# A new engine order for attention with beacon keys and a two-layer MLP, from a planner with longer delays for the beacon keys

## The chip, the cores and the metric

The kernel runs on one core of a Trainium2 chip. What counts is the device time of one execution in microseconds; of several executions of one kernel the median is taken. A profile is one further execution, recorded by the hardware profiler.

## The reference, cut to what matters

Eight batches of eight heads attend over 576 tokens of width 64. In front of the keys and values stand 16 beacon keys and values that every query sees; the rest is causal. The attention's output, 4608 tokens of width 512, goes through two dense layers with a sigmoid-gated unit between them.

```python
k_all = np.concatenate([beacon_k, k], axis=2)
v_all = np.concatenate([beacon_v, v], axis=2)
scores = scale * np.matmul(q, k_all.transpose(0, 1, 3, 2))
causal[:, Nb:] = np.triu(np.ones((S, S), dtype=bool), k=1)
scores = np.where(causal, -1000000000.0, scores)
scores = scores - scores.max(-1, keepdims=True)
a = np.exp(scores)
a /= a.sum(-1, keepdims=True) + 1e-09
x = np.matmul(a, v_all)              # then (tokens, 512)
h = x @ w_in                         # (4608, 512) @ (512, 2048)
g = h * (1.0 / (1.0 + np.exp(-1.702 * h)))
out = g @ w_out                      # (4608, 2048) @ (2048, 512)
```

All inputs are float32 and are turned to float16 as they are loaded; the output is float32.

## The kernel before, in words

**Steps.** Four heads of one batch make a step `s`; there are 16 steps, two for each batch. A step loads its q and k (GpSimd DMA, L349), turns both on VectorE so that the head's width lies on partitions (`e_turn`: L398 for the beacon keys, L405 for k and q), multiplies them in chunks on TensorE (`qk`, L434), takes exps on ScalarE (L445), sets what causality hides to zero on GpSimd or VectorE (L466, L459), multiplies with a matrix of ones and with the values (`av`, L521), and divides by the sums on VectorE (z1 L533, z2 L540 and L544, norm L556). Steps 0 and 1 are early steps: their chunks are cut so that a first half of the tokens is done before the second. There is one score tile, so a chunk's matmuls wait for the exps of the chunk before. All other PSUM results share a ring of four banks.

**Beacon keys.** They are float32 in `bkf`, which is set to zero first, then filled by DMAs of SyncE (a few of ScalarE for step 0), and cast for each step into `bkn` by VectorE (`e_bk`, L390). The loads for step 0 and step 1 are issued at once. Those for steps 2 and 3, 4 to 7 and 8 to 15 each follow a memset (L1072, operations 82, 87 and 92 of the plan), and are four DMAs each. SyncE also issues the output's stores, all in one order.

**Dense layers.** Tokens go in groups of 256 or 512. The first layer (`m1`, L580) is followed by tanh and a gate (L594, L613) in groups 0 and 1, by one activation (L601) later. The second layer is plain in groups 0 and 1 (`m2`, L625). Groups 2 to 9 form seven products of quarter matrices (L694) from sums of quarters made on VectorE (`s`, L645) and join them (L705, L710). The weights are loaded in pieces by GpSimd, at most eight of its loads in flight at a time.

**The order.** Nothing is scheduled at run time. The kernel makes a list of operations, each with an engine, a planned duration and dependencies. `ORDER`, a table of numbers, gives for each engine the order in which its operations stand. `Plan.run` walks through the table with planned durations and delays (`Plan.lat`) and so decides which ring bank each result gets and in which order the code is emitted. The table comes from a search made beforehand with the same durations and delays. Each engine works through its list in order and waits where a dependency isn't met.

The numbers that matter here. TensorE: 76, 100, 106, 108, 111, 129, 131, 134 are `qk0` to `qk7` (steps 0 and 1), 227 is `qk8`, the first of step 2; 115, 118, 120 are the values of step 0, first half, and 138, 141, 143 those of step 1; 122, 125, 127 and 145, 148, 150 are the second halves; 152, 155, 158 and so on are first-layer blocks of group 0; 176 and 177 the first second-layer blocks. VectorE: 73, 97, 224, 255, 398, 411 cast the beacon keys of steps 0 to 5; 74 and 75 turn k and q of step 0, 98 and 99 those of step 1, 225 and 226 those of step 2; 82, 87, 92 are the memsets; 126 and 128 are norms of step 0's second half, 149 and 151 of step 1's; 347 is the first join of group 2.

Of the kernel before, what the change touches and what calls it, by code (L numbers as in the profile page):

```python
# [17 lines left out]
        76, 100, 115, 118, 120, 106, 138, 143, 141, 108, 152, 111, 155, 158, 129, 161, 122, 164, 131, 167, 170, 134,  # L18
        127, 125, 173, 176, 145, 148, 150, 177, 182, 188, 191, 227, 194, 197, 183, 232, 203, 200, 234, 178, 179,
        237, 184, 206, 258, 241, 209, 185, 263, 212, 213, 265, 248, 253, 251, 246, 268, 214, 215, 401, 218, 272,  # L20
        279, 244, 404, 277, 219, 220, 407, 282, 284, 275, 221, 414, 312, 292, 306, 435, 308, 316, 302, 310, 320,
        304, 300, 290, 296, 294, 298, 318, 314, 423, 426, 343, 338, 339, 349, 344, 340, 341, 345, 438, 346, 431,
        429, 433, 464, 350, 365, 351, 359, 360, 574, 354, 355, 356, 352, 361, 577, 366, 357, 477, 362, 367, 583,
        474, 368, 372, 373, 374, 605, 480, 482, 484, 375, 607, 488, 504, 498, 610, 494, 516, 486, 490, 496, 500,
        492, 510, 508, 506, 512, 502, 514, 593, 596, 534, 535, 539, 536, 545, 540, 537, 546, 550, 742, 551, 552,
        541, 542, 547, 745, 599, 548, 603, 601, 619, 622, 748, 553, 555, 561, 556, 557, 755, 558, 562, 625, 627,
        629, 776, 563, 564, 568, 569, 570, 764, 767, 779, 571, 657, 649, 661, 651, 653, 635, 659, 647, 641, 631,
        637, 805, 770, 772, 774, 633, 643, 645, 639, 655, 684, 690, 679, 685, 680, 686, 681, 682, 915, 815, 818,
        691, 692, 687, 695, 700, 918, 693, 696, 701, 702, 697, 924, 698, 703, 821, 823, 825, 946, 706, 707, 708,
        709, 713, 948, 934, 937, 714, 715, 716, 827, 951, 944, 940, 942, 841, 829, 855, 853, 849, 845, 839, 851,  # L30
        857, 835, 833, 831, 837, 843, 847, 1083, 960, 963, 875, 880, 876, 881, 877, 878, 882, 1086, 970, 966, 968,
        883, 1089, 896, 886, 887, 888, 891, 1096, 892, 893, 902, 894, 889, 1117, 897, 903, 898, 899, 904, 1120, 909,
        910, 905, 911, 1105, 1108, 1146, 912, 986, 992, 994, 990, 976, 982, 974, 988, 1000, 978, 984, 972, 980, 998,
        1002, 996, 1256, 1156, 1115, 1111, 1113, 1159, 1025, 1026, 1020, 1021, 1022, 1023, 1259, 1031, 1027, 1028,
        1166, 1162, 1164, 1265, 1032, 1033, 1041, 1034, 1042, 1043, 1287, 1036, 1037, 1038, 1039, 1044, 1289, 1275,
        1278, 1054, 1055, 1047, 1048, 1049, 1050, 1056, 1292, 1281, 1283, 1285, 1057, 1198, 1196, 1182, 1168, 1184,
        1172, 1170, 1178, 1174, 1176, 1180, 1188, 1190, 1301, 1304, 1194, 1192, 1216, 1186, 1307, 1221, 1222, 1223,
        1339, 1217, 1218, 1227, 1224, 1228, 1229, 1219, 1232, 1230, 1337, 1243, 1233, 1237, 1238, 1234, 1239, 1244,
        1235, 1240, 1245, 1246, 1309, 1311, 1250, 1319, 1251, 1329, 1252, 1325, 1335, 1321, 1315, 1253, 1419, 1323,
        1411, 1423, 1421, 1331, 1343, 1333, 1313, 1415, 1341, 1403, 1429, 1409, 1361, 1362, 1363, 1364, 1413, 1327,  # L40
        1317, 1407, 1417, 1401, 1366, 1367, 1431, 1405, 1388, 1368, 1369, 1427, 1382, 1383, 1425, 1377, 1378, 1389,
        1372, 1373, 1374, 1390, 1391, 1375, 1384, 1385, 1379, 1380, 1395, 1396, 1397, 1454, 1398, 1455, 1470, 1471,
        1456, 1472, 1449, 1473, 1450, 1451, 1452, 1460, 1461, 1462, 1457, 1463, 1465, 1466, 1467, 1468, 1476, 1477,
        1478, 1479, 1483, 1484, 1485, 1486,
    ],
    "ACT": [
        1, 3, 77, 79, 101, 103, 107, 109, 153, 112, 156, 159, 130, 162, 165, 132, 168, 171, 135, 174, 189, 192, 228,
        195, 198, 233, 201, 235, 204, 238, 180, 207, 259, 210, 264, 186, 266, 269, 216, 402, 405, 408, 222, 415,
        417, 293, 309, 313, 303, 311, 307, 305, 317, 291, 321, 297, 301, 295, 299, 319, 315, 436, 342, 439, 465,
        468, 575, 578, 587, 584, 606, 608, 489, 505, 517, 487, 491, 499, 501, 493, 497, 511, 495, 507, 513, 509,  # L50
        503, 515, 611, 538, 743, 746, 749, 756, 758, 777, 780, 658, 650, 654, 662, 636, 660, 652, 632, 642, 638,
        648, 806, 634, 644, 646, 640, 656, 809, 683, 916, 919, 925, 928, 947, 949, 952, 828, 830, 842, 850, 856,
        840, 846, 858, 836, 834, 852, 854, 838, 832, 844, 848, 1084, 879, 1087, 1090, 1099, 1097, 1118, 1121, 1150,
        1147, 987, 991, 993, 995, 983, 975, 1001, 979, 989, 985, 981, 977, 1003, 973, 997, 999, 1257, 1024, 1260,
        1266, 1269, 1288, 1290, 1293, 1199, 1197, 1183, 1169, 1185, 1179, 1171, 1175, 1173, 1177, 1181, 1189, 1191,
        1193, 1195, 1187, 1340, 1220, 1338, 1320, 1326, 1330, 1322, 1336, 1324, 1316, 1412, 1422, 1424, 1332, 1420,
        1344, 1334, 1314, 1404, 1430, 1416, 1342, 1414, 1365, 1318, 1408, 1328, 1418, 1410, 1432, 1402, 1406, 1428,
        1426, 1453,
    ],
    "DVE": [  # L60
        73, 97, 74, 75, 98, 99, 78, 81, 80, 116, 117, 102, 121, 104, 105, 119, 139, 140, 144, 142, 154, 157, 123,
        124, 82, 160, 166, 163, 169, 172, 224, 126, 128, 175, 146, 147, 149, 151, 225, 226, 87, 190, 193, 196, 255,
        199, 256, 257, 205, 202, 411, 286, 398, 208, 287, 242, 211, 243, 399, 249, 400, 250, 252, 254, 247, 92, 412,
        280, 273, 281, 413, 245, 274, 278, 283, 276, 285, 288, 461, 419, 580, 463, 289, 462, 330, 420, 331, 421,
        332, 322, 422, 323, 333, 326, 427, 327, 424, 334, 335, 324, 336, 428, 425, 337, 328, 347, 329, 325, 432,
        430, 470, 434, 582, 471, 472, 473, 353, 581, 358, 478, 363, 475, 476, 479, 369, 370, 481, 483, 485, 589,
        739, 590, 376, 752, 741, 753, 615, 591, 754, 740, 522, 523, 518, 802, 519, 592, 520, 524, 921, 525, 526,
        527, 594, 521, 530, 528, 531, 597, 595, 532, 529, 616, 617, 598, 533, 543, 618, 600, 549, 604, 620, 602,
        623, 554, 621, 624, 760, 559, 761, 628, 762, 630, 763, 626, 565, 768, 566, 765, 572, 769, 811, 812, 803,
        766, 804, 922, 773, 771, 671, 775, 923, 663, 1093, 664, 665, 667, 813, 814, 668, 675, 672, 676, 669, 666,  # L70
        673, 816, 670, 819, 674, 820, 688, 1080, 677, 694, 817, 678, 930, 699, 704, 931, 822, 932, 933, 824, 826,
        710, 935, 938, 939, 936, 711, 717, 945, 943, 941, 956, 957, 958, 1082, 1081, 1094, 959, 1095, 859, 1262,
        863, 871, 860, 864, 865, 961, 867, 964, 965, 962, 872, 861, 868, 873, 869, 971, 866, 884, 1143, 862, 969,
        870, 874, 967, 1101, 1144, 890, 1145, 1102, 1103, 1104, 895, 900, 1109, 1106, 906, 913, 907, 1152, 1153,
        1107, 1263, 1154, 1264, 1012, 1155, 1008, 1110, 1013, 1014, 1009, 1157, 1116, 1016, 1112, 1010, 1004, 1160,
        1114, 1005, 1161, 1006, 1158, 1011, 1017, 1029, 1167, 1018, 1007, 1015, 1019, 1271, 1035, 1272, 1163, 1165,
        1273, 1274, 1040, 1276, 1279, 1045, 1280, 1277, 1051, 1052, 1284, 1286, 1058, 1282, 1297, 1298, 1200, 1299,
        1300, 1204, 1201, 1305, 1205, 1306, 1302, 1303, 1202, 1308, 1206, 1212, 1213, 1208, 1209, 1214, 1203, 1215,
        1225, 1207, 1210, 1211, 1231, 1236, 1241, 1247, 1248, 1310, 1312, 1254, 1357, 1349, 1350, 1345, 1358, 1359,
        1351, 1353, 1360, 1354, 1352, 1355, 1346, 1356, 1347, 1348, 1370, 1376, 1381, 1386, 1392, 1393, 1437, 1441,  # L80
        1433, 1434, 1438, 1399, 1435, 1442, 1445, 1446, 1436, 1443, 1439, 1444, 1440, 1447, 1448, 1458, 1464, 1469,
        1474, 1480, 1481, 1487,
    ],
    "POOL": [
# [32 lines left out]
class Plan:  # L117
# [69 lines left out]
    def lat(self, d, o):  # L187
        if o.eng == "Q":
            return 300 if d.eng == "SP" else 1200
        if d.name == "bk" and d.eng != "DVE":  # L190
            return 2500
# [928 lines left out]
```

## Time and profile before

| | |
|---|---|
| median of three executions | 333.64 us |
| their lowest and highest | 332.74, 335.28 us |
| profiled execution | 336.76 us, of which the span from the first to the last instruction is 335.1 us |
| busy, TensorE matmul | 313.5 us (94%), 4288 instructions |
| busy, VectorE, ScalarE, GpSimd | 234.9 (70%), 201.2 (60%), 112.8 us (34%) |
| DMA | 28.81 MB |

The page names engines PE (TensorE), PEld (its weight loads), DVE (VectorE), ACT (ScalarE), POOL (GpSimd) and SP (SyncE). In its second part the span is cut into 40 slices of 8.4 us; a digit is the busy share in tenths, and the row PEclk is the share of TensorE's clock that was granted. The chain that ended last is followed back from the last instruction. In a timeline, a line gives the start, the length, the engine, the source line and the operation, and in brackets how long the engine had been idle and what ended that. In the list of waits, a line gives who waited for whom, the time in total, how often, and the longest.

The DMA row of the slices is at 9 for most of the first 67 us and seldom later: the inputs of the first steps and all weights are loaded there.

```profile
DMA  7999999939051980199019909810110001000023
```

### The profile page before, as it was taken

What the parts mean: (1) busy time and instruction counts of PE and PEld (TensorE: products, weight loads), DVE (VectorE), ACT (ScalarE), POOL (GpSimd) and SP (SyncE); (2) the same over time, 40 slices, a digit from 0 to 9 for tenths busy, and PEclk for the clock granted to TensorE, in tenths of its full rate; (3) what the DMA queues carried; (4) which work ended last, traced back from release to release, by engine and by line L of the source; (5) the groups of instructions that cost most, each with busy time, mean ns of one, the idle gap of its engine ahead of it and who ended that gap; (6) DMA issues with size and microseconds to landing.
All of it is one profiled execution on the core that took longest, in us unless ns stands there. A gap on an engine that the chain in (4) does not pass through costs nothing. (4 is left out here: it accounts for less than half of the span.)

```text
span 335.1 us, 9823 instructions
## 1 busy us (share of the span) xinstructions
PE 313.5 (94%) x4288; PEld 212.2 (63%) x4288; DVE 234.9 (70%) x478; ACT 201.2 (60%) x236; POOL 112.8 (34%) x178
## 2 busy tenths in 40 slices
PE   0499699999999999999999999999999999999995
PEld 0377376654687457755778877646874586455884
DVE  0755658886999879977897979777983844006294
ACT  1378069876976777577967696767666422645100
POOL 8746537637034803481048108320303000000000
PEclk9999699999999999999999999999999999999999
DMA  7999999939051980199019909810110001000023
GB/s 125 162 205 209 196 98 169 117 85 165 0 106 64 147 101 25 45 138 139 2 67 100 178 3 89 127 59 3 33 65 33 2 31 65 32 0 2 31 97 125
DMA packets 58219, 28.81 MB, mean 86 GB/s; under 512 B 41280, under 2 KB 53568, under 8 KB 58176
## 3 DMA queue, kind: packets, MB, share of 16 engines
q0 software_dynamic: 47552, 18.49, 47.5%
q1 hardware_dynamic: 10560, 9.69, 8.8%
q8 instruction: 33, 0.54, 0.7%
q14 instruction: 10, 0.08, 0.1%
q10 hardware_dynamic: 64, 0.01, 0.0%
HBM read 37.22 MB, written 9.44 MB: 139 GB/s over the span
## 5 line engine op out<-in xcount | busy, mean ns | idle before, releaser
L580 PE MATMUL u<-xT,w 128*128 128x512 f16 (+1 forms) x704 | 131.1, 341 | 0.1
L445 ACT ACTIVATE E<-s 128x2048 f16<-128x2048 f32 (+4 forms) x66 | 98.9, 1514 | 46.5 <-PE s L434 46.3
L580 PEld LDWEIGHTS <-w 128*128 128x128 f16 x704 | 67.8, 98 | 53.6 <-issue 1.0
L601 ACT ACTIVATE g<-u 128x512 f16<-128x512 f32 x128 | 69.8, 599 | 46.1 <-PE u L580 45.9
L466 POOL TENSOR_SCALAR_AFFINE_SELECT E<-E 128x512 f16<-128x512 f16 (+3 forms) x78 | 48.1, 644 | 127.7 <-ACT E L445 118.7
L694 PEld LDWEIGHTS <-g 128*128 128x128 f16 x512 | 48.7, 98 | 7.7
L710 DVE SCALAR_TENSOR_TENSOR osb<-u,osb 128x512 f32<-128x512 f32 x56 | 37.4, 681 | 20.2 <-PE u L694 16.4
L694 PE MATMUL u<-w,g 128*128 128x256 f16 x384 | 49.2, 273 | 0.0
L434 PE MATMUL s<-qT,kT 32*128 32x32 f16 (+20 forms) x1376 | 35.7, 234 | 14.2 <-DVE kT L398 11.2
L434 PEld LDWEIGHTS <-kT 32*128 32x128 f16 x1376 | 26.1, 95 | 30.9 <-issue 13.1
L694 PEld LDWEIGHTS <-sA 128*128 128x128 f16 x384 | 36.1, 98 | 6.1 <-issue 0.2
L694 PE MATMUL u<-tB,sA 128*128 128x256 f16 x256 | 34.3, 273 | 0.0
L645 DVE TENSOR_TENSOR sA<-g 128x512 f16<-128x512 f16 x32 | 13.1, 417 | 28.0 <-ACT g L601 27.9
L521 PE MATMUL u<-E,vb 128*32 128x352 f16 (+8 forms) x928 | 28.9, 273 | 0.0
L556 DVE TENSOR_TENSOR xT<-u,rz 128x352 f16<-128x352 f32 (+2 forms) x52 | 26.0, 518 | 3.1 <-PE u L521 2.5
L365 POOL DMA_DIRECT2D vb<-in_v_dram x32 | 27.4, 875 | 1.6 <-DMA qn<-in_q_dram 0.8
L521 PEld LDWEIGHTS <-vb 128*32 128x32 f16 (+1 forms) x928 | 21.1, 101 | 6.0 <-issue 1.7
L484 DVE TENSOR_TENSOR zs<-zs,E 128x1344 f16<-128x1344 f16 (+2 forms) x36 | 22.5, 626 | 3.0 <-POOL E L466 2.1
L405 DVE STREAM_TRANSPOSE kT<-kn 128x576 f32<-128x576 f32 x16 | 20.1, 1257 | 3.4 <-PE s L434 1.9
L484 DVE TENSOR_TENSOR zs<-E 128x1856 f16<-128x1856 f16 x12 | 15.4, 1282 | 9.4 <-POOL E L466 9.4
L533 DVE STREAM_TRANSPOSE zt<-u 128x224 f32<-128x224 f32 (+2 forms) x32 | 14.8, 473 | 7.6 <-PE u L521 7.4
L405 DVE STREAM_TRANSPOSE qT<-qn 128x576 f32<-128x576 f32 x16 | 19.7, 1234 | 0.0
(44 smaller groups left out, 241.1 us busy)
## 6 DMA issues: line engine op xcount, KB each, us to landing
out_dram<-osb SPq DMA_DIRECT2D x36, 256.0 KB, 2.5
kn<-in_k_dram POOLq DMA_DIRECT2D x16, 288.0 KB, 6.9
qn<-in_q_dram POOLq DMA_DIRECT2D x16, 288.0 KB, 6.8
vb<-in_v_dram POOLq DMA_DIRECT2D x24, 128.0 KB, 5.9
w<-in_moe_w_in_dram POOLq DMA_DIRECT2D x8, 256.0 KB, 8.1
w<-in_moe_w_out_dram POOLq DMA_DIRECT2D x4, 512.0 KB, 13.1
vb<-in_v_dram POOLq DMA_DIRECT2D x8, 112.0 KB, 4.0
vb<-in_v_dram POOLq DMA_DIRECT2D x8, 80.0 KB, 6.9
```

The costliest lines, as they stand in the source:

```text
L365: nc.gpsimd.dma_start(out=t[0 : hi - lo, j, h0:h1, :], in_=v[b, h0:h1, lo:hi, :].rearrange("h n d -> n h d"),)
L405: nc.vector.transpose(out=f32(dst.rearrange("p n e -> p (n e)")).rearrange("p (r t) -> p t r", t=TR), in_=f32(src[:, :]).rearrange("p (t c ...
L434: nc.tensor.matmul(sc[:, h, o : o + w], kT[s % NB2][r : r + 32, j * P : (j + 1) * P, d], qT[s % NB2][r : r + 32, a : a + w, d], start=(d = ...
L445: nc.scalar.activation(out=Es[s][:, :, c0:c1], in_=ss[i][:, :, o : o + c1 - c0], func=AFT.Exp, scale=0.125,)
L466: nc.gpsimd.affine_select(out=blk, in_=blk, compare_op=ALU.is_ge, fill=0.0, base=off + (Nb if j == 0 else 0), pattern=[[0, Q], [1, w]], ch ...
L484: nc.vector.tensor_tensor(out=t, in0=E[:, :, Z0:S] if i == 1 else t, in1=E[:, :, wcol[i] : wcol[i] + S - a], op=ALU.add,)
L521: nc.tensor.matmul(u[32 * h : 32 * h + 32, a:e], lhs, src[0:kw, h, col : col + e - a], start=first, stop=last,)
L556: nc.vector.tensor_tensor(out=xT[:, 2 * hs + x : 2 * hs + x + n, t0 : t0 + w], in0=rings[("av", s, x, half)][:, 0 : n * w].rearrange("p (n ...
L580: nc.tensor.matmul(u[:, o + a - t0 : o + e - t0], w1t[:, kp, nt * P : (nt + 1) * P], xT[:, kp, a % XR : (e - 1) % XR + 1], start=(kp == 0) ...
L601: nc.scalar.activation(out=gts[g][:, n0:n1, 0:w], in_=rings[("m1", g, n0)][:, 0 : n * w].rearrange("p (n w) -> p n w", n=n), func=AFT.Gelu ...
L694: nc.tensor.matmul(u[:, HM * mt : HM * (mt + 1)], lhs[:, n, mt * P : (mt + 1) * P], rhs[:, n, :], start=(n == 0 and mt == 0), stop=(n == H ...
L710: nc.vector.scalar_tensor_tensor(out=osbs[(g, dst)][:, :], in0=rings[("p", g, p)][:, :], scalar=scale_of(g), in1=osbs[(g, src)][:, :], op0 ...
```

## The change

In `Plan.lat`, the planned delay between a load of beacon keys and their cast was 2500 ns for every step. It becomes 2500 for step 0, 5200 for step 1 and 9000 for the later ones. `ORDER` is replaced by a table that the search found with these delays. SyncE's list is the same in both; TensorE's, ScalarE's, VectorE's and GpSimd's differ from the start to the end, with the same operations in each. GpSimd's loads keep their order; its masks swap places with their neighbours. Of the table the first rows of TensorE and VectorE are shown, the rows in which memset 92 stands, and VectorE's last.

```diff
     "PE": [
-        76, 100, 115, 118, 120, 106, 138, 143, 141, 108, 152, 111, 155, 158, 129, 161, 122, 164, 131, 167, 170, 134,
-        127, 125, 173, 176, 145, 148, 150, 177, 182, 188, 191, 227, 194, 197, 183, 232, 203, 200, 234, 178, 179,
+        76, 100, 106, 138, 115, 141, 118, 143, 120, 108, 111, 155, 152, 129, 161, 158, 122, 131, 164, 167, 134, 127,
+        170, 173, 176, 145, 125, 148, 150, 177, 182, 188, 191, 227, 194, 197, 232, 183, 203, 234, 200, 178, 237,
...
     "DVE": [
-        73, 97, 74, 75, 98, 99, 78, 81, 80, 116, 117, 102, 121, 104, 105, 119, 139, 140, 144, 142, 154, 157, 123,
-        124, 82, 160, 166, 163, 169, 172, 224, 126, 128, 175, 146, 147, 149, 151, 225, 226, 87, 190, 193, 196, 255,
-        199, 256, 257, 205, 202, 411, 286, 398, 208, 287, 242, 211, 243, 399, 249, 400, 250, 252, 254, 247, 92, 412,
...
-        1433, 1434, 1438, 1399, 1435, 1442, 1445, 1446, 1436, 1443, 1439, 1444, 1440, 1447, 1448, 1458, 1464, 1469,
-        1474, 1480, 1481, 1487,
+        73, 74, 75, 97, 98, 99, 80, 81, 82, 78, 105, 87, 104, 102, 139, 116, 117, 121, 119, 140, 144, 142, 157, 154,
+        123, 163, 160, 124, 224, 169, 128, 166, 172, 175, 146, 147, 126, 149, 151, 225, 226, 398, 190, 193, 196,
...
+        421, 322, 92, 323, 324, 422, 427, 428, 424, 425, 325, 330, 334, 329, 335, 432, 336, 331, 434, 337, 332, 333,
...
+        1399, 1437, 1434, 1438, 1447, 1435, 1441, 1442, 1436, 1443, 1444, 1439, 1448, 1440, 1458, 1464, 1469, 1480,
+        1474, 1481, 1487,
...
         if d.name == "bk" and d.eng != "DVE":
-            return 2500
+            return {"bk0": 2500, "bk1": 5200}.get(o.name, 9000)
         return self.LAT[d.eng] if o.eng != d.eng or d.eng == "Q" else 0
```

## The prediction

> **What bounds the kernel now.** I began with the page: the busy time of the engines (PE 313.5 of 335.1 us), the slices with the clock row, and the chain that ended last, which is PE alone from 212.75 us on. In the slices the reader is to see that the first two hold idle PE, that the fifth is a 6 in PE's row and in the clock's, and that nothing else is short of 9 before the last slice:
>
> ```profile
> PE   0499699999999999999999999999999999999995
> ...
> PEclk9999699999999999999999999999999999999999
> ```
>
> Sums by stretch say the same: from 42 to 331 us PE is busy 288.39 of 289.00. So time can be won only before 42 us or in the tail of 4 us. Next I asked who PE waited for. Before 40 us there are three entries; after 40 us there is one, of 0.2 us:
>
> ```profile
> PE s L434 <- DVE kT L398: 11.2, 1, 11.2
> PE u L521 <- DVE xT L556: 3.0, 1, 3.0
> PE s L434 <- ACT E L445: 2.8, 3, 2.0
> ```
>
> The releasers of the first two stand in DVE's timeline, and in both places a cast of beacon keys (L390) is the instruction that DVE stood at. The brackets give the idle time before it and what ended it:
>
> ```profile
> 8.51 0.20 DVE L390 CAST bkn<-bkf 128x64 f16<-128x64 f32 x1 [4.68 <-DMA bkf<-in_beacon_k_dram]
> ...
> 9.96 1.23 DVE L405 STREAM_TRANSPOSE qT<-qn 128x576 f32<-128x576 f32 x1
> ...
> 27.92 0.17 DVE L1072 MEMSET bkf<- 128x128 f32 x1
> ...
> 35.78 0.20 DVE L390 CAST bkn<-bkf 128x64 f16<-128x64 f32 x1 [4.36 <-DMA bkf<-in_beacon_k_dram]
> ```
>
> The second place costs more than its wait. PE stands still from 33.3 to 36.4 us and then runs at half clock; the columns after the stretch are its length, PE, PEld, DVE, ACT and POOL busy, granted clock, DMA share and GB/s:
>
> ```profile
> 33.30:35.40 2.10, 0.07 (x1) 0.09 (x1) 0.00 (x0) 0.00 (x0) 2.10 (x3) 1.00 1.14 207
> 35.50:36.40 0.90, 0.01 (x2) 0.01 (x2) 0.62 (x3) 0.00 (x0) 0.46 (x2) 0.50 1.20 204
> 36.40:38.90 2.50, 2.50 (x52) 2.01 (x55) 2.08 (x5) 0.00 (x0) 1.31 (x2) 0.50 1.24 207
> 38.90:42.30 3.40, 3.40 (x23) 1.24 (x15) 3.21 (x5) 0.00 (x0) 0.56 (x1) 0.50 1.89 174
> 42.30:44.40 2.10, 2.10 (x20) 1.58 (x19) 0.55 (x3) 0.60 (x1) 0.00 (x0) 1.00 2.25 173
> ```
>
> PE lost 3.03 us of standstill and half of the 5.9 us from 36.4 to 42.3: 2.95. Together 5.98 us.
>
> **The Trainium skill.** "TensorE: Matmul & The Clock Gate", Part 1: the array's clock is halved by default and after an idle window of about 3.4 us; a busy window of that length restores it; the windows run free of the kernel. The trace agrees: half clock from about 35.4 to 42.3 us is two such windows, and at the start the matmuls are slow (24 of scores 1.04 us at 11.24, 0.54 at 24.51). A stretch from 14.9 to 18.4 us with PE busy 2.86 of 3.50 did not end it, one from 18.4 to 21.8 with 3.24 of 3.40 did. "Perfetto Trace Analysis", Tensor Engine Instruction: VectorE's queue is strictly in order, so what is behind a waiting cast waits too; the norms that release PE at 36.39 do. "DMA: Bandwidth & Descriptors", Issuing engines are not separate DMA queues: SyncE's transfers share 16 engines with GpSimd's. In the trace the first beacon loads land 1.6 to 1.8 us after their issue, the next, behind the loads of q and k, after 3.9 to 5.1, those of 28 us after 4.4 to 6.2.
>
> **The change, part by part.** No instruction is added or removed. The planner's delay between beacon load and cast changes from 2.5 us for all to 2.5, 5.2 and 9 (step 0, step 1, later), and with it the order on PE, ACT, DVE and POOL; SP's order and that of GpSimd's loads among themselves stay.
>
> *Cast of bk1 behind the turns of step 0.* k0 and q0 land at 1.30+4.4=5.7 and 1.96+5.1=7.1 us, so the turn of q0 (1.23 us) ends at about 8.4 instead of 11.2. qk0 starts at 8.5, not 11.24: 2.75 earlier. bk1 (landed 8.39) is then cast with no wait. q1 lands at 2.99+7.6=10.6, its turn ends at 11.9, and qk1 starts at 11.95, not 14.32: 2.37 earlier.
>
> *What PE does with that.* qk2 now comes before the values of half 0, and must wait for the exps of qk1 (1.94 us, one score tile): 11.95+1.04+0.05+1.94 gives 15.0; it ran at 17.40. The six value groups follow; the old ones took 15.29 to 16.76 for three, so 2.85 for six, to 18.9. qk3 runs at 19.05, its exp from 19.9 to 21.4 (1.45). qk4 now stands directly behind qk3 and must wait for that exp, where the old order had one first-layer block in between. So qk4 starts at 21.4, or 20.9 if full clock came at 18.4: I take 21.2 against 22.18. But the old order had by then done one block more, worth 0.93 (two take 22.66 to 24.51, 1.85). The lead of 2.4 us shrinks to 1.0 in time and to nothing in work done. I book 0, between +1 and -1.
>
> *Memsets of bkf at 12 to 15 us instead of 27.92 and 42.44.* They cost 0.17 and 0.27 us on DVE, which then waits for scores anyway. SyncE issues their eight loads by about 17 us, in place of 28 to 30 and 43 to 45; with 6 us to land they are there by 23. Their 96 KB at 205 GB/s take 0.5 us from the weight loads next to them; the weights that land at 11.6+7.2=18.8 and 20 us are read after 24, so this is hidden. Cast bk2 then runs near 29 us without a wait, and bk4 too.
>
> *The stretch from 33 us.* Everything that PE does before the values of step 1, half 1 is the same work as before, except that one value group (0.5 us) now stands behind them. They start at 33.3-0.5-0.1 = 32.7, if their bank's norm is done: it is behind one gate whose tanh ends near 29.6. The first two parts of the second-layer weights land at 17.2+11.8=29.0 and 18.0+13.2=31.2, before their use. The four groups take 20 and 60 matmuls at full clock (0.68 for 20 over ones, 1.18 for 40 over values): 2.2 us, to 34.9. Two second-layer blocks of 4 matmuls (the chain has 4 such in 0.86) take 1.75, to 36.7. Old: 42.5. The two first-layer blocks then take 1.85, to 38.6; DVE needs norms until 36.1 and the turns of step 2 until 38.6 (k2, q2 landed by 22.6+10=32.6 and 34.2). qk8 starts at 38.7, not 44.39: a gain of 5.7.
>
> *The rest.* Behind qk8 PE has no slack, so the lead is kept if the new order is as dense. The numbers of changes between the three tile forms (scores, values, dense) are 148 before, 145 after; with 0.21 us idle before the weight load each, 0.3 to 0.6 gained, most of it before qk8 and counted above. In the tail, one join of the last group now follows another after PE's next to last product: 3 joins take 1.9 us beside 2.2 us of matmuls; cost 0 to 0.3. I take 0.3 lost.
>
> Sum: 0 + 5.7 - 0.3 = 5.4; less 0.2, since the standstill in other executions meets the windows at another place (half clock 3.4 to 6.8 us, of which this one had 5.9 us at work). 5.2. Against its own span 335.1 gives 329.9. That execution took 336.76 us, above all three others (332.74 to 335.28), so I take the difference from the median: 333.64-5.2 = 328.4.
>
> **Unknown costs.** The start's clock: from 15.0 to 19.9 us PE is dense for 4.9 us, then idle up to 1.5. A window of 3.4 us fits in there in some 6 of 10 placements; otherwise full clock comes only at 25 to 28 us, and 5 or 6 us of work are done at half rate: 2 to 3.7 us lost. The bulk's new order: below nothing to 2 us; a gain is excluded, as 0.6 us are all that PE idles there.
>
> **Rivals.**
> 1. Late clock at the start, as just priced: 328.4+3.1 = 331.5. For it: the new gap ahead of qk4. Against: the denser stretch before it. 0.25.
> 2. The wait for keys is replaced at 33 us by another: masks of step 1 on POOL follow qk7's exp, which ends near 31; k2/q2, second-layer rows. If PE still idles 2 us with half clock half the time: gain 2 to 3, 331.5 to 332. For it: DMA is full there (207 GB/s). Against: those landings preceded their use before. 0.10.
> 3. Slower: the third memset (128x512) moves from 64.56 to behind the first sums of group 2, near 86 on the old clock. On SP, behind its loads (2.76 us of issue), stand three output stores that went at 67.93; the first join of group 2 (93.23) needs a store's buffer. 86.5+2.8+0.1 = 89.4 to issue; landing 1.9 to 5.9 (the store of 93.95 took 5.9) gives 91.3 to 95.3. Held 2.1 us, the join costs PE up to 2. The point is 3 us: from there PE would drop to half clock as at 36 and lose 6 us, more than the gain, 334.4; held 5 us it loses 8.5: 337. 0.07.
> 4. The start keeps its 2.4 us because full clock comes early: 326. 0.08.
>
> **How the numbers follow.** The forecast itself, 327 to 330, has 0.50. 328.4 is its time. The range leaves out the lower half of case 4, most of 3 and the top of 1 and 2: 326.2 to 332.8. One per cent of 333.64 is 3.3 us, about what runs that spread over 2.5 us can tell. Faster by more: nearly all of the forecast, case 4 and a quarter of case 1, 0.64. Within: 0.29. Slower: 0.07.
>
> **What would show it.** DVE idle at L390 below 1 us in both places; qk0 at 8.5 us; PE without a gap of over 1 us from 22 to 42 us; clock 1.00 throughout that stretch; qk8 near 38.7; PE busy over 99.5% from there. It is wrong if clock 0.5 stands beyond 25 us, if PE waits for DVE or ACT by over 1 us behind 42 us, or if the join of group 2 waits for a store.

## The result, and the profile after

| | before | after |
|---|---|---|
| median (lowest, highest) of 4 executions each | 333.32 us (332.74, 335.28) | 330.08 us (329.79, 330.55) |
| profiled execution, its span | 336.76, 335.1 us | 329.79, 328.1 us |
| granted clock, mean of the profiled execution | 0.990 | 1.000 |
| PE busy | 313.5 us | 309.3 us |

The medians differ by 3.24 us, 0.97%. The ratio on record, worked out from all executions, is 0.9894, with a 95% interval of 0.9851 to 0.9937; so four executions each do not decide whether the gain is above or below 1%. The forecast was 328.4 us, with 5.2 us of gain. Profile against profile the difference is 7.0 us. So the first question on this result is which of the two differences the reasons have to explain.

The slices of the page after: the 6 in the fifth slice of PE and of its clock is gone.

```profile
PE   0489999999999999999999999999999999999995
...
PEclk9999999999999999999999999999999999999999
```

The waits of PE after, up to 42 us (who waited for whom, total us, times, longest us). The 3.0 us for `xT` is no longer among them; the wait for qk0's inputs now ends with q's turn and is 2.8 us shorter; the waits for exps grew from 2.8 to 5.7.

```profile
PE s L434 <- DVE qT L405: 8.4, 1, 8.4
PE s L434 <- ACT E L445: 5.7, 3, 2.0
```

DVE's timeline after (start us, us, line and operation, then idle time before it and what ended it). The cast of step 1 now stands behind the turn of q and idles 0.22 us instead of 4.68. The memset stands at 12.08 us instead of 27.92, and the cast of step 2 has no bracket: it waited for nothing.

```profile
7.07 1.26 DVE L405 STREAM_TRANSPOSE qT<-qn 128x576 f32<-128x576 f32 x1
8.55 0.20 DVE L390 CAST bkn<-bkf 128x64 f16<-128x64 f32 x1 [0.22 <-DMA bkf<-in_beacon_k_dram]
...
12.08 0.17 DVE L1072 MEMSET bkf<- 128x128 f32 x1
...
27.73 0.19 DVE L390 CAST bkn<-bkf 128x64 f16<-128x64 f32 x1
```

PE's timelines show where that time goes. Before, from the standstill on:

```profile
36.39 1.15 PE L521 MATMUL u<-E,ones 128*32 128x288 f16 x20 [3.03 <-DVE xT L556]
...
39.40 3.32 PE L625 MATMUL u<-w,g 128*128 128x512 f16 x8
...
44.39 0.64 PE L434 MATMUL s<-qT,kT 32*128 32x288 f16 x24
```

After, qk0 starts at 8.38, the values of step 1's second half at 31.39 without a wait, the second-layer blocks take 1.90 us instead of 3.32, and qk8, from which the rest of the kernel is counted here, starts at 37.24 instead of 44.39.

```profile
8.38 1.04 PE L434 MATMUL s<-qT,kT 32*128 32x288 f16 x24 [8.38 <-DVE qT L405]
...
20.01 0.55 PE L434 MATMUL s<-qT,kT 32*128 32x208 f16 x32 [1.58 <-ACT E L445]
...
31.39 0.68 PE L521 MATMUL u<-E,ones 128*32 128x288 f16 x20
...
33.50 1.90 PE L625 MATMUL u<-w,g 128*128 128x512 f16 x8
...
37.24 0.64 PE L434 MATMUL s<-qT,kT 32*128 32x288 f16 x24
```

Sums by stretch of after (stretch, length, busy PE, PEld, DVE, ACT, POOL, granted clock, DMA share, GB/s). The clock is 1.00 through the stretch that was at half clock before. In the last line PE is busy 286.13 of 287.00 us; the same work took 286.80 us in the profile before (44.4 to 331.2). So all 7.15 us by which qk8 is earlier are won ahead of it, and the new order of the rest is worth nothing: from qk8 to the end of the execution it is 292.37 us before (336.76 less 44.39) and 292.55 after.

```profile
30.40:33.50 3.10, 3.10 (x87) 2.11 (x85) 2.68 (x6) 0.60 (x1) 1.26 (x2) 1.00 1.11 210
33.50:37.20 3.70, 3.64 (x32) 2.35 (x25) 3.50 (x8) 0.62 (x2) 2.65 (x3) 1.00 1.15 207
37.20:324.20 287.00, 286.13 (x3796) 192.10 (x3795) 211.47 (x424) 183.47 (x216) 88.08 (x133) 1.00 0.49 75
```

### The profile page after: what moved, and what is told of

Same layout as the page of the kernel before. It is cut to its first block, busy times and chain, and to the rows that moved or that the text cites. A ratio compares the mean times of both kernels' runs of the same rounds, so it can differ in the third digit from the quotient of the medians.

```text
span 328.1 us, 9811 instructions
## 1 busy us (share of the span) xinstructions
PE 309.3 (94%) x4288; PEld 210.0 (64%) x4288; DVE 235.9 (72%) x478; ACT 202.0 (62%) x236; POOL 114.0 (35%) x178
## 4 chain that ended last, share of the span: by engine, by line
PE 89%; ACT 4%; DVE 3%; DMA 2%; issue 1%; POOL 0%; DVEq 0%; ACTq 0%; POOLq 0%
PE u L580 36%; PE u L694 30%; PE s L434 9%; PE u L521 9%; PE u L625 4%; ACT E L445 3%; DMA qn<-in_q_dram 2%; DVE qT L405 1%; DVE sA L645 1%; DVE xT L556 1%; DVE rz L544 0%; DVE zt L533 0%; ACT L601 0%; DVE osb L710 0%; DVE rc L540 0%
## 5 line engine op out<-in xcount | busy, mean ns | idle before, releaser
L445 ACT ACTIVATE E<-s 128x2048 f16<-128x2048 f32 (+5 forms) x66 | 98.9, 1515 | 46.0 <-PE s L434 45.6
L466 POOL TENSOR_SCALAR_AFFINE_SELECT E<-E 128x512 f16<-128x512 f16 (+3 forms) x78 | 49.3, 663 | 113.4 <-ACT E L445 81.6
L694 PE MATMUL u<-w,g 128*128 128x256 f16 x384 | 50.6, 273 | 0.0
L694 PE MATMUL u<-tB,sA 128*128 128x256 f16 x256 | 35.0, 273 | 0.1
L521 PE MATMUL u<-E,vb 128*32 128x352 f16 (+8 forms) x928 | 28.0, 267 | 0.0
L521 PEld LDWEIGHTS <-vb 128*32 128x32 f16 (+1 forms) x928 | 20.2, 99 | 5.9 <-issue 1.7
```

Of the source, the lines that this page charges most:

```text
L445: nc.scalar.activation(out=Es[s][:, :, c0:c1], in_=ss[i][:, :, o : o + c1 - c0], func=AFT.Exp, scale=0.125,)
L466: nc.gpsimd.affine_select(out=blk, in_=blk, compare_op=ALU.is_ge, fill=0.0, base=off + (Nb if j == 0 else 0), pattern=[[0, Q], [1, w]], ch ...
L521: nc.tensor.matmul(u[32 * h : 32 * h + 32, a:e], lhs, src[0:kw, h, col : col + e - a], start=first, stop=last,)
L694: nc.tensor.matmul(u[:, HM * mt : HM * (mt + 1)], lhs[:, n, mt * P : (mt + 1) * P], rhs[:, n, :], start=(n == 0 and mt == 0), stop=(n == H ...
```

## The experiments

Two theories stood at the outset of why the profiled execution of before took 3 us more than the others, and so of what the keys cost in the usual one. **A**: every execution has the standstill of 3 us near 33 us, and they differ in the half clock that follows it. **B**: the landing of the keys varies, and with it the standstill; then the usual execution loses less there, and the start must carry a part of the gain. Most edits below are small changes of the order on VectorE; the numbers are those of the table `ORDER`, and its rows are cut short on the right.

### The kernel before again, and how its executions differ

Unchanged, so that its own spread and a second profile are there.

> The kernel before, once more, to see what the profiled execution of 336.76 us had that the others (332.74 to 335.28) had not. Theory A, the half clock varies: the standstill near 33 us is in every execution, but it meets the clock windows at another place each time; executions near 333 us show a mean granted clock of 1.00, one of 335 or more shows 0.99 (6.8 us at half clock of 335), and the new profile, if near 333, shows the cast waiting 4 to 5 us and less than 3 us of work at half clock. Theory B, the landing varies: in a fast execution the cast of step 2 waits 1 to 2 us only and PE stands still for under 1 us.

Measured: 334.64 us in the median of 22 executions (332.98 to 336.38), beside 333.81 of 48 further ones (332.49 to 336.78), ratio 1.0015 (0.9992 to 1.0039). Ordered by their mean granted clock they fall apart: of these 22, eleven have 0.998 or more and take 332.98 to 334.15 us, eleven have 0.993 to 0.995 and take 335.12 to 336.38. The profile is of the second kind: 335.94 us at 0.994, with a standstill of 3.0 us again. Two more executions were profiled, to see one of each kind.

> The kernel before again, for a trace of an execution of the faster kind (three in four are). If it comes at clock 1.00 and about 333 us, theory A expects the same standstill of 3.0 us (33.3 to 36.4) with matmuls at full rate behind it, and the first chunk of step 2 near 41.5 to 42.5 instead of 44.4 and 43.6 us in the two traces so far. Theory B expects a standstill of under 1.5 us.

> As the run before this one: one more trace of the same kernel, since which kind it is cannot be chosen. A trace at clock 0.99 shows 3.4 or 6.8 us of half clock behind the standstill; one at 1.00 none.

They took 333.33 us (clock 0.998) and 335.70 us (clock 0.995). PE's timeline of the first:

```profile
35.38 0.68 PE L521 MATMUL u<-E,ones 128*32 128x288 f16 x20 [1.55 <-DVE xT L556]
...
36.98 1.90 PE L625 MATMUL u<-w,g 128*128 128x512 f16 x8
...
40.91 0.64 PE L434 MATMUL s<-qT,kT 32*128 32x288 f16 x24 [0.28 <-DVE qT L405]
```

and of the second:

```profile
36.51 0.68 PE L521 MATMUL u<-E,ones 128*32 128x288 f16 x20 [3.19 <-DVE xT L556]
...
38.39 3.25 PE L625 MATMUL u<-w,g 128*128 128x512 f16 x8
...
43.32 0.64 PE L434 MATMUL s<-qT,kT 32*128 32x288 f16 x24
```

In the first the standstill is half as long and the clock does not drop behind it: the two second-layer blocks take 1.90 us, as after the change. Two things make it shorter. PE comes to it 0.5 us later (at 33.83, against 33.32 in the second), because the matmuls of the start stayed slow for longer there (eight of the first layer took 1.94 us from 20.64 on, in the second 1.32 from 20.51). And the last of the four loads of keys for steps 2 and 3 lands earlier. The four land 4.5 to 4.8 us after their issue in the first (the last at 34.64 us), 4.5 to 6.4 in the second (35.77), 4.4 to 6.2 in the profile that the prediction used. DVE's timeline of the first has the cast at 34.76, a microsecond earlier than the 35.78 of that profile:

```profile
34.76 0.49 DVE L390 CAST bkn<-bkf 128x64 f16<-128x64 f32 x1 [2.88 <-DMA bkf<-in_beacon_k_dram]
```

Put together, with the time from the first value group of step 1's second half to qk8 as the measure of what the half clock costs:

| execution of before | clock | standstill | first value group to qk8 | half-clock windows | lost |
|---|---|---|---|---|---|
| 333.33 us | 0.998 | 1.6 us | 35.38 to 40.91: 5.53 | 0 | 1.6 us |
| 335.70 us | 0.995 | 3.2 us | 36.51 to 43.32: 6.81 | 1 | 3.2 + 1.3 = 4.5 us |
| 335.94 us (b_again) | 0.994 | 3.0 us | 36.83 to 43.55: 6.72 | 1 | 3.0 + 1.2 = 4.2 us |
| 336.76 us (the prediction's) | 0.990 | 3.0 us | 36.39 to 44.39: 8.00 | 2 | 3.0 + 2.5 = 5.5 us |

From qk8 to the end all four take the same, 292.37 to 292.42 us, so their differences arise ahead of it. In the second and the last row the loss differs from that of the first by 0.5 us more than the times do, since PE came to the standstill 0.5 us later in the first (and in b_again, whose difference fits).

Of 124 executions of before that ran in these experiments, 80 have a mean clock of 0.997 or more, 38 of 0.993 to 0.995, and 6 of 0.990. By the table these are executions with no window, one and two; most of them have no trace. The share of those with windows differs between series (11 of 48, 11 of 22, 8 of 27, 14 of 27). So the profiled one is of the rarest kind, one in twenty, and the usual one loses 1.6 us, as far as one trace of it tells. A's standstill of 3 us in every execution and its qk8 at 41.5 to 42.5 were missed (1.55 us, 40.91). B holds in that the landing varies; the half clock comes on top in the costly kinds. Why the fourth load lands late in some executions stays open. Three of the four profiles of before are of costly kinds, where 44 of the 124 executions are; whether the recording itself has a part in this was not tested.

### One move at a time

First, in the order before, only the cast of step 1's keys put behind the turns of step 0 (b_cast):

```diff
     "DVE": [
-        73, 97, 74, 75, 98, 99, 78, 81, 80, 116,
+        73, 74, 75, 97, 98, 99, 78, 81, 80, 116,
```

> The order before with the cast of bk1 behind the turns of step 0 alone. qk0 at 8.4 us instead of 11.2, qk1 near 11.5. The prediction's account of the start (lead kept only where PE finds work) says: here, unlike in the new order, a first-layer block still stands between qk3 and qk4, so the lead of 2.4 us reaches 22 us whole, but the wait for the keys of step 2 stays, and because their memset comes earlier by the same 2 us, so does their landing: 1.5 to 2.5 us faster than before. A rival, that the loads set the pace at 33 us: nothing gained, within 0.5 us.

Measured: 332.62 us (330.24 to 335.75, 22 executions), ratio to before, without the longest, 0.9946 (0.9923 to 0.997): 1.2 us faster by the medians, less than expected. Its list of PE's waits, up to 42 us, still has the standstill, and its executions still fall apart by clock (330.24 to 332.36 at 0.998 or more, 332.50 to 335.75 below):

```profile
PE s L434 <- DVE qT L405: 10.8, 2, 8.7
PE u L521 <- DVE xT L556: 3.2, 1, 3.2
PE s L434 <- ACT E L445: 1.1, 3, 0.6
```

Comparing executions without half-clock windows, a median of 331.1 us stands against 333.4 of before: the earlier start brings 2.3 us. That is what was expected of the old order, in which a first-layer block stands between qk3 and qk4; the prediction's 0 was for the start of the new order.

Second, only the memset for the keys of steps 2 and 3 put forward, and with it their loads (b_mem):

```diff
     "DVE": [
-        73, 97, 74, 75, 98, 99, 78, 81, 80, 116,
+        73, 97, 74, 75, 98, 99, 78, 81, 80, 82, 116,
...
-        124, 82, 160, 166,
+        124, 160, 166,
```

> The order before with memset 82 alone moved behind the first three masks, so that the keys of steps 2 and 3 load at 15 us. Cast of step 2 without a wait, no standstill near 33 us, start as before (qk0 at 11.2). If this part alone made the change's gain, 3 us faster than before, 330.3; if it is worth what the profile of before showed, 5 to 6 us, 328; if another wait takes its place, under 1 us.

Measured: 331.58 us (331.13 to 332.14, 11 executions), ratio 0.9929 (0.9902 to 0.9956): 2.2 us faster than the median of all of before's executions, 1.8 faster than those without half-clock windows (about 333.4). All eleven have a clock of 0.997 or more, and they spread over 1.0 us in place of 4.3. That is none of the three sizes expected; it fits the usual standstill of 1.6 us, and no execution of the costly kinds is left.

Third, both together (b_both):

> Both small edits on the order before, none of the rest of the new table. If the rest of the new order is worth nothing, equal to the changed kernel (330.1) within 0.7 us; if the first-layer block between qk3 and qk4 keeps the lead of the start, 1 to 2 us faster than it, 328 to 329; if the rest of the new order is what gains, slower than 331.

Measured: 329.54 us (329.31 to 329.61, 6 executions), ratio 0.9866 (0.9829 to 0.9903), 4.3 us faster. The list of PE's waits, up to 60 us, shows both gone, and one short new one, before second-layer matmuls at 55.92 us:

```profile
PE s L434 <- DVE qT L405: 9.0, 2, 8.8
PE s L434 <- ACT E L445: 2.8, 3, 2.0
PE u L625 <- issue: 0.7, 1, 0.7
...
```

Against the usual 333.4 us of before these are 3.9 us, beside 1.8 for the memset alone and 2.3 for the cast alone: the two nearly add up. Two operations moved in the old order thus give everything that the new table of all operations gives.

### The half clock by itself

To separate the wait from the clock, the standstill of before was filled with matmuls whose results nobody reads (b_warm):

```diff
-        127, 125, 173, 176, 145, 148, 150, 177,
+        127, 125, 173, 176, 1489, 145, 148, 150, 177,
...
+    def e_warm():
+        sc = pss.tile([P, Q, 512], F32, tag="s", name="s")
+        for i in range(14):
+            nc.tensor.matmul(sc[:, i % Q, :], w1t[:, 0, 0:P], w1t[:, 0, 512:1024], start=True, stop=True)
...
```

> The order before with 14 matmuls of 128x512 on weights (3.0 us at full clock, their results read by nobody, an addition to the work) put on TensorE into the standstill at 33 us, behind the first second-layer block. The cast still waits for its keys, so the 3 us stay lost. Theory A (two kinds of executions, apart by the half clock after the standstill): granted clock at least 0.997 in all, no execution above 335, median where the faster kind of the kernel before lies, 333 to 333.5, so 0.3 to 0.8 below its median. Theory B (apart by the landing of the keys): both kinds stay.

Measured: 334.70 us (334.27 to 335.16, 14 executions), beside 335.10 of before (332.67 to 337.31, 27 executions, 14 of them with half-clock windows); ratio 0.9987 (0.9962 to 1.0011). The 333 to 333.5 of theory A was missed. All fourteen executions are at a clock of 0.999 or 1.000, so the dropping of the clock is indeed due to PE's standing still. But the filling takes its 3.0 us in every execution, also where the keys would have come after 1.6. It removes the costly kinds of before (335.1 to 337.3) and spoils its usual one (332.7 to 334.6).

### The two moves undone in the kernel after

In the new order, only memset 82 put back behind the first gates (a_memlate). SyncE issues its loads in one order, so the four loads for steps 4 to 7, which follow, go late with it: all eight are issued from 27.28 us on.

```diff
-        73, 74, 75, 97, 98, 99, 80, 81, 82, 78, 105, 87, 104, 102, 139, 116, 117, 121, 119, 140, 144, 142, 157, 154,
-        123, 163, 160, 124,
+        73, 74, 75, 97, 98, 99, 80, 81, 78, 105, 87, 104, 102, 139, 116, 117, 121, 119, 140, 144, 142, 157, 154,
+        82, 123, 163, 160, 124,
```

> The changed kernel with memset 82 alone moved back, behind the first gates (its load then starts near 25 us, 3 us ahead of the cast in place of 15). The early memset as the cause: the cast of step 2 waits 4 to 6 us again, TensorE stands still for 3 to 4 us and in part of the executions falls to half clock: 333 to 336, median 3 to 5 us over the changed kernel. If the rest of the new table had made the gain: within 1 us of 330.1.

Measured: 334.95 us (333.04 to 337.10, 14 executions), ratio to before 1.0002 (0.9971 to 1.0033). By the medians the whole gain is gone. Its four fastest executions, at a clock of 1.000, take 333.04 to 333.64 us, some 3 us more than after; of the other ten nine have a clock of 0.987 to 0.995, and one, at 1.000, takes 334.65 us, perhaps by the late clock of which the next part tells. Its profile (clock 0.995) has the cast of step 2's keys waiting again in DVE's timeline,

```profile
33.47 0.39 DVE L390 CAST bkn<-bkf 128x64 f16<-128x64 f32 x1 [3.39 <-DMA bkf<-in_beacon_k_dram]
```

and PE at half clock behind it, by the sums of that stretch:

```profile
34.40:37.70 3.30, 3.30 (x12) 1.48 (x11) 2.10 (x4) 0.60 (x1) 2.12 (x3) 0.50 1.21 202
```

PE stands still for 2.3 us there, for a first-layer block whose gate is queued behind the cast on DVE; in the order before it was the value group. qk8 is at 43.65, 6.4 us later than after: 2.3 from the start, whose full clock came late in this execution (qk7 at 29.86 instead of 27.59), 2.3 of standstill, and about 1.8 that remain for the window at half clock.

In the new order, only the cast of step 1's keys put back before the turns of step 0 (a_castfirst):

```diff
-        73, 74, 75, 97, 98, 99, 80,
+        73, 97, 74, 75, 98, 99, 80,
```

> The changed kernel with the cast of bk1 alone put back ahead of the turns of step 0. qk0 returns to 11.2 us. The prediction's step (the new order makes nothing of the early start) would leave the time as it is, within 1 us of the changed kernel. The trace of the changed kernel says that 1.5 us of the lead were still there at 37 us: 1.5 to 2.7 us slower than it, 331.5 to 332.7, one kind of execution.

Measured: 333.34 us (332.49 to 336.20, 22 executions), ratio to before 0.9978 (0.9954 to 1.0003); 3.1 us slower than after beside it (330.25), more than the 1.5 to 2.7 expected. Nor are the executions of one kind: fourteen take 332.49 to 333.44 us, eight 334.35 to 336.20, all at a clock of 0.999 or 1.000; none of the eight was profiled. The profile has qk0 3.2 us later than after, and qk8 3.6 us later: in this order nothing on the way takes up the delay. PE's timeline:

```profile
11.60 1.04 PE L434 MATMUL s<-qT,kT 32*128 32x288 f16 x24 [11.60 <-DVE kT L398]
...
40.80 0.64 PE L434 MATMUL s<-qT,kT 32*128 32x288 f16 x24
```

So within the new order the place of the cast is worth 3.1 us, and without it the new order is no faster than before (333.50 beside it), though its memset is early. The expectation took this run for a test of the prediction's 0, which it is not: that 0 was for the early cast and the new order on PE together, and its steps from qk1 to qk4 are a chain, which a later qk1 shifts whole.

### The late clock at the start

The kernel after, unchanged (a_again), and b_both again (b_both2) beside it.

> The changed kernel again, beside the two small edits on the order before, for a comparison on one chip: 329.8 to 330.6, no second kind of execution, since nothing in it stands still long enough to drop the clock.

> Both small edits on the order before, again. If it beats the changed kernel, 0.3 to 0.8 us less than it, no second kind of execution; if the earlier 329.54 was the chip's or the day's, equal within 0.3.

After took 330.25 us in the median of six: four at 330.08 to 330.26, two at 332.09 and 332.21; ratio to before 0.9878 (0.982 to 0.9936). That there would be no second kind of it did not hold. The profile is of the second kind, and PE's timeline shows rival 1 of the prediction: 24 matmuls of scores take 0.83 us at 18.41 where they took 0.54 at 17.90 in the other profile, and 16 of the first layer 3.14 where they took 1.92. So the full clock came at about 24 us instead of 17.7. It has to be read from the lengths of matmuls, as the clock column says 1.00 from the start on.

```profile
18.41 0.83 PE L434 MATMUL s<-qT,kT 32*128 32x192 f16 x24
...
20.80 0.83 PE L434 MATMUL s<-qT,kT 32*128 32x208 f16 x32 [1.56 <-ACT E L445]
21.56 3.14 PE L580 MATMUL u<-xT,w 128*128 128x256 f16 x16
...
39.54 0.64 PE L434 MATMUL s<-qT,kT 32*128 32x288 f16 x24
```

qk8 is at 39.54, 2.3 us behind the 37.24 of the other profile, of which 0.4 us were there at qk0 already. Over both series of after two executions of ten are that long; one of them has a trace.

A dense stretch was not enough. The first two lines are this execution, the third is the first profile of after:

```profile
14.97:18.40 3.43, 3.43 (x96) 2.60 (x95) 1.98 (x5) 1.45 (x1) 2.25 (x4) 1.00 1.71 183
17.20:20.60 3.40, 2.04 (x60) 1.57 (x53) 2.80 (x9) 1.41 (x2) 1.74 (x3) 1.00 1.26 200
14.30:17.70 3.40, 3.15 (x92) 2.53 (x95) 2.01 (x6) 1.64 (x2) 2.05 (x3) 1.00 1.72 182
```

Here PE was busy without a break from 14.97 to 18.40 us, and stayed slow. If windows of 3.4 us are counted back from where the full clock came, the figures fit: in the window just ahead of it PE was busy 3.15 of 3.40 us in the first profile of after, 3.20 here (20.60 to 24.00) and 3.24 in the prediction's profile of before; in the windows before those it was 1.04, 2.04 and 2.76. Here the dense stretch was split between two windows. That the windows lie so is worked out from these figures, not recorded.

b_both2 took 329.66 us (329.24 to 330.01), ratio 0.9849 (0.9799 to 0.99). All six of its executions are below all six of after: 0.6 us by the medians, and none of the second kind. In b_both's first profile qk8 is at 36.36, 0.9 us ahead of after, and the short wait at 55.92 us takes 0.7 of it back. The order before with two operations moved has the lowest median of this study.

Last, an attempt to have the full clock from the first scores on (b_prewarm): b_both, with 16 matmuls on a constant tile before qk0 and 6 between qk0 and qk1, whose results nobody reads.

```diff
-        76, 100, 115, 118, 120, 106,
+        1489, 76, 1490, 100, 115, 118, 120, 106,
...
+    def e_warm(n):
+        u = ring_tile(("warm", 0))
+        for _ in range(n):
+            nc.tensor.matmul(u[:, :], wz[:, 0:P], wz[:, :], start=True, stop=True)
...
```

> Both small edits, and TensorE kept busy from 1.5 us with 16 matmuls of 128x512 on a constant tile, and 6 more between qk0 and qk1, results read by nobody (an addition to the work). If the slow matmuls up to 18 to 23 us cost time (the half clock of the start), qk0 to qk2 and the first values take half, and the time falls by 1 to 2 us against the two edits alone, 327.5 to 328.5. If the start is bound by loads and exps, within 0.5 us of them. If the 22 matmuls overrun qk0 or qk1: up to 1 us slower.

Measured: 330.14 us (328.98 to 330.96, 6 executions), ratio 0.9861 (0.9809 to 0.9913): no gain over b_both, and within the 0.5 us expected if loads and exps bind the start. In its profile the full clock is there from 4.9 us and the scores of step 0 take 0.64 us instead of 1.04, but then PE waits in turn for first-layer weights (its line numbers are two higher, for the added code):

```profile
21.17 0.83 PE L582 MATMUL u<-xT,w 128*128 128x256 f16 x6 [0.68 <-DMA w<-in_moe_w_in_dram]
```

Three of the six have a clock of 0.994 or 0.995, as before has with one half-clock window; where it lies is not known, since the profile is of another execution.

## Why the prediction was right, and where it was not

The measured 330.08 us lies in the range. The gain was 3.24 us where 5.2 was forecast, so by the medians it stayed just inside the 1%, to which I had given 0.29. The steps:

**Cast of bk1 behind the turns: right.** qk0 was put at 8.5 and ran at 8.38; qk1 at 11.95 and ran at 11.47; DVE idles 0.22 us at that cast.

**Memsets and loads moved forward: right.** The loads were issued from 12.3 to 15.6 us, landed by 21.7 (I had said 23), and the casts wait for nothing. Pieces of the first-layer weights land up to 1.4 us later than before, but PE never waited for them.

**The stretch from 33 us: right in what happens.** From the first value group to qk8 it took 5.85 us where my steps gave 6.0. The size of the gain is what failed: 3.03 us of standstill and 2.95 of half clock. The half clock cost 2.5 us in that execution, by the table above, where I had half of 5.9; 0.28 us of the difference is a wait for a turn on VectorE that stands ahead of qk8 at full clock. And that execution was the wrong one to take the sum from: the usual one loses 1.6 us and no clock, so 5.98 stood where it has 1.6. I had seen that it took 336.76 us, above all the others shown, and wrote "so I take the difference from the median". The step that failed is this one. I took 0.2 off the sum for other places of the windows, as though the standstill itself were the same in every execution. The excess of 3.1 us over the median was the wait and the clock that I was counting as gain.

**The start, booked at 0: wrong, on the other side.** I let the lead of 2.4 us vanish by qk4 ("to nothing in work done"). Measured, qk4 ran at 20.01 instead of the 21.2 that I took. Of these 1.2 us, 0.5 were there at qk1, and nearly 0.7 come from the way from qk1 to qk3, which took 6.43 us where my steps gave 7.1. The clock has little part in that: with the late clock this way took 6.52. Behind qk4 the full clock, there since 17.7 us, kept the lead. The first value group of step 1's second half then ran at 31.39 instead of 32.7, and 1.3 us of the 1.46 by which qk8 was early come from there. With the late clock that group ran at 33.69, 1.0 us later than 32.7. So against the profile that I used, the start was worth 1.3 us or -1.0, by when the full clock came; against the usual execution of before, whose own start was 0.5 us slower, 1.8.

Taken together, for the usual execution of before: 1.6 us of standstill, 1.8 us at the start, and 0.3 of its wait for a turn ahead of qk8. That is about the 3.67 us between its qk8 (40.91) and that of after (37.24), and the 3.54 between these two executions (333.33 and 329.79). The medians give 3.24. So two errors partly cancelled: too much for the wait by 4.2 us (5.98 less 0.2, against 1.6), too little for the start by about 2. That the time lies well within the range is in this part luck.

**The rest and the tail.** "As dense" held: 287.0 us against 286.8. The 0.3 us that I took as lost in the tail did not occur: PE's last matmul ends some 3.9 us before the span's end in both profiles.

**The rivals.** Rival 1, the late clock, is there in one traced execution and, by its time, in a second, of ten; it costs 1.9 us, priced at 3.1. Rival 2, another wait at 33 us: none. Rival 4, a start that keeps its 2.4 us because full clock comes early, was the nearest to what happens in the other eight, of which one has a trace; its 326 was too low since it kept the 5.7 us. Rival 3, the join of group 2 held up by a store behind SP's loads: the memset was moved to 77.99 us, the loads went out from 78.50 to 80.23 and the stores landed by 83.81, so the join, at 89.44, had nothing to wait for; DVE idled 0.28 us before it, and not for a DMA.

## What to carry to other kernels

One profile is one execution: before a wait in it is turned into a gain, compare its time and its mean granted clock with those of the other executions, and if it stands out, price the wait from one that does not. Before a whole new order is taken over, try the few operations in it that remove a wait which the profile names: here two moved operations came to more than a new table of all. A bound on the start of a kernel has to be given for an early and for a late full clock, since here two executions of the same kernel differed in it by 6 us.

## What the hardware showed that I had not expected

- The clock does not drop after every standstill. In the order before, PE idle for 3.0 or 3.2 us was followed by one or two windows of 3.41 us at half clock (in the profile of 335.70 us from 37.75 to 41.16); idle for 1.6 us was not. In the new order with the memset put back, an idle time of 2.3 us before 34.3 was enough. So the window of about 3.4 us that halves the clock need not be idle throughout, as the prediction's wording has it: in the 3.41 us ahead of the four drops PE was busy for 0.50, 1.09, 1.24 and 1.31 us.
- Whether one window of half clock follows or two goes with the work in the first. In the profile that the prediction used PE was busy for 2.49 of its 3.41 us, because the standstill reached into it, and a second followed; in the profiles of 335.70 and 335.94 us it was busy for 3.41 and 3.32, and the full clock came back.
- At the start, 3.43 us with PE busy throughout (14.97 to 18.40 us in the second profile of after) did not bring the full clock, where a window with 3.15 of 3.40 in the first profile did: by these traces it matters where the windows lie, and two executions of one kernel differ in that.
- Four loads of keys, issued within 1.3 us of each other beside other loads (some 207 GB/s in all), land after 4.4 to 6.4 us, where the first loads of the kernel needed 1.6 to 1.8; and the last of them varies by over 1 us from one execution to the next.
